# A four-layer FNet and GeGLU kernel in split fp32: the planner's price of short DMA packets, a normalisation begun one step earlier, and another layout of stored weight pieces

## Chip, cores and metric

The kernel runs on one core of a Trainium2 chip. The metric is the device time of one execution in microseconds. Before the change three runs took 1600.6, 1602.94 and 1600.12 us, a median of 1600.6 us. A profile of one more execution, which itself took 1600.54 us, is the source of all rows below.

## The reference

The input x has 2048 rows of 512 fp32 numbers. Four layers follow one another, each on the layer-normed rows of the last:

```python
x = x + _A_ref(_layernorm(x), ...)   # Cr @ (z Hr) - Ci @ (z Hi), the real part of a 2-D DFT
x = x + _B_ref(_layernorm(x), ...)   # (gelu(z @ w_gate) * (z @ w_up)) @ w_down
x = x + _A_ref(_layernorm(x), ...)
x = x + _B_ref(_layernorm(x), ...)
```

Cr and Ci are 2048 x 2048, Hr and Hi 512 x 512, w_gate and w_up 512 x 1792, w_down 1792 x 512. `_layernorm` subtracts the row's mean and divides by the root of its variance plus 1e-5.

## The kernel before, in words

**Arithmetic.** Each fp32 operand is divided into a high part rounded to fp32r (`split`, L121 on ScalarE, called ACT) and a rest (L123 on VectorE, called DVE). A product is three TensorE (PE) matmuls, high by high, high by rest, rest by high (`mm3`, L161 to L163). Large products go by a Strassen scheme with seven operands in place of eight, named A11, A12, S1, S2, S3, S4 and A22; their sums and differences are the DVE lines L149 and L152.

**Stages.** Layers 0 and 2 (`mix`) go over four blocks b of 512 output rows, first all products with the sequence matrices (`fore`, S2, S4), then the products with the hidden matrices (`hid_groups`); in layer 2 blocks 2 and 3 do the latter together (`pair_products`). Layers 1 and 3 (`geglu`) go twice, for w = 0 and w = 1, over 1024 rows each: 14 steps `up(n)` of seven products make gate and up, then the products with w_down follow. A product in `up` is six matmuls and calls `step()` once.

**Buffers.** All tiles of 128 x 512 come from 93 slots handed out in turn (`sb`, named s in the profile); two wide tiles, `wide` and `xwide`, hold four such tiles each and serve at times as slots, at times for turned rows. PE writes to eight PSUM banks (p).

**Weights that are kept.** Weight sums are made once, divided, and stored to DRAM by POOL (GpSimd's queue), so that later passes load them ready. `weight_steps` makes four pieces for each block of gate and up (DRAM tiles wb), of w_down (wc, `wdd`) and of the paired hidden matrices (wp, `whd`). A piece is a pair of operands such as S2 and S3, each of 256 columns: `split_slot` makes one tile with both operands' high parts and one with both rests, and `kept` (L274) stores these two tiles one behind the other, 2 KB a row each. A w_down or wp load (`piece_of`, L262, issued by SyncE's queue, SP, at L293) wants one operand, high and rest, so it reads two runs of 1 KB a row. The loads of wb (`piece_load`, L1021) take the whole tiles as they were stored. The fourth piece holds S4 alone, high beside rest. w_down's blocks 0 to 2 are made in the first mix layer beside block 0's hidden products, the others in the first GeGLU pass (`up`, L1090); wh's own pieces (whs) are stored by `kept` as well.

**Normalisation.** In layer 0 the terms come from DVE and one POOL instruction (L511); in the others `norm_terms` has ACT sum and square the row (L518 to L520), POOL make 1/root (L521, L522) and ACT the shift (L523); then L540 on ACT writes the normalised row. For the GeGLU layers `block_steps` does this for eight tiles of 128 rows per w: `norm(i)` loads rows ahead (`x_load_mixed`, L198, SP), normalises tile i, lets DVE transpose it into `wide` (L624), and after each fourth tile POOL stores `wide` to DRAM (t, L627); `fetch` (L638) loads it back in runs of 512 bytes. For w = 0 these steps run as chores beside the hidden products of blocks 1 and 2 (in layer 2 of block 2's as queue entries); for w = 1 they lie in `slow`, of which every ninth `step()` runs one (PACE), during the GeGLU pass for w = 0. `terms_ahead` makes the terms alone for layer 2's first rows, with the scratch tile `junk`.

**Turned rows.** `load_turned` (L229, SP) loads rows of x into `wide` or `xwide` in runs of 512 bytes, products are added to them, and `rows_done` (L242, POOL) stores them.

**Order.** The code's order is a priority; which instruction stands where on each engine is fixed at build time by a planner that runs a timing model of the machine. `machine_as_traced` sets four of that model's constants from traces: the gap between matmuls, SP's delay, the depth of the issue queues, and 21.5 bytes per ns for each DMA engine. At run time each engine and each queue works in the planned order and waits at its head.

Of the kernel before, what the change touches and what calls it, by code (L numbers as in the profile page):

```python
# [9 lines left out]
F32 = mybir.dt.float32  # L10
# [4 lines left out]
P = 128  # L15
S, D, F = 2048, 512, 1792
# [5 lines left out]
NT = TB // P  # L22
# [28 lines left out]
SP_DELAY_NS = 3000  # L51
DEPTH = 1
DMA_BYTES_PER_NS = 21.5


@with_exitstack
def fnet_geglu(ctx: ExitStack, tc: tile.TileContext, x_in, ws, wh, whc, wgu, wdc, out):
    nc = tc.nc
# [5 lines left out]
    tpool = ctx.enter_context(tc.tile_pool(name="turned", bufs=1))  # L64
# [11 lines left out]
    junk = cpool.tile([P, D], F32, name="junk")  # L76
# [36 lines left out]
    sb = Slots(slots, "s", NSLOT)  # L113
    ps8 = Slots(psum, "p", 8)

    def f32(ap):
        return ap.bitcast(F32)
# [74 lines left out]
    def x_load_mixed(layer, i):  # L192

        g, n = divmod(i, NT)
        t = sb.get()
        for j in range(NT):
            r0 = j * P + n * 32
            nc.sync.dma_start(t[j * 32:(j + 1) * 32], xs[layer, g][r0:r0 + 32])  # L198
        return t
# [62 lines left out]
    def piece_of(place, k, name):  # L262

        i = next(i for i, names in enumerate(pieces) if name in names)
        needs[len(items)] = place[k].name, i
        if i == 3:
            return place[k][:, 3 * 1024:]
        h = half[pieces[i].index(name)]
        return place[k][:, i * 1024:(i + 1) * 1024].rearrange("p (h c) -> p h c", h=2)[:, :, h]

    def halves(t):
        return t[:, :512], t[:, 512:]

    def kept(place, parts):  # L274
        for t, a in zip(parts, halves(place)):
            nc.gpsimd.dma_start(a, f32(t))  # L276


    items, needs, outside = [], {}, set()
# [1 line left out]
    raws, parts = {}, {}  # L281
# [206 lines left out]
    known, terms_made = {}, []  # L488

    def row_of(layer, i, mixed):  # L490
        x = fresh.pop(("mixed", i) if mixed else i, None)
        if x is None:
            x = (x_load_mixed if mixed else x_load)(layer, i)
        return x
# [31 lines left out]
    def terms_ahead(layer, i, n):  # L526
# [6 lines left out]
        known[layer, i] = norm_terms(layer, i, x, junk)  # L533
        sb.put(x)

    def normed(layer, i, mixed=False):
        x = row_of(layer, i, mixed)
        z = sb.get()
        rstd, shift = known.pop((layer, i), None) or norm_terms(layer, i, x, z)
        nc.scalar.activation(z, x, AF.Identity, bias=shift, scale=rstd)  # L540
        sb.put(x)
        return z
# [5 lines left out]
    def first_norm(layer, k):  # L548
        za[k] = normed(layer, k)
# [56 lines left out]
    def block_steps(layer, w):  # L606

        zt, t, wide = {}, {}, {}
        turned = [dram.tile([P, NT * D], F32, name=f"t{layer}_{w}_{part}") for part in range(2)]

        def norm(i):

            def run():
                r0 = w * 2 * NT
                end = 2 * NT if w else i // NT * NT + NT
                for k in range(i if i == 0 or i + NT == end and not w else i + 2, min(i + 3, end)):
                    fresh["mixed", r0 + k] = x_load_mixed(layer, r0 + k)
                z = normed(layer, r0 + i, True)
                part, n = divmod(i, NT)
                if n == 0:  # L620
                    assert not sb.out("z")
                    wide[part] = tpool.tile([P, NT * D], F32, name="wide")
                to = wide[part].rearrange("p (b n t) -> p b n t", n=NT, t=32)
                nc.vector.transpose(to[:, :, n], z.rearrange("p (b t) -> p b t", t=32))  # L624
                sb.put(z)
                if n == NT - 1:
                    nc.gpsimd.dma_start(turned[part], wide.pop(part))  # L627
            return run

        def fetch(c):  # L630

            def run():
                for part in range(2):
                    v = zt[c, part] = sb.get()
                    for i in range(P // 32):
                        cols = turned[part][:, (c * 4 + i) * P:(c * 4 + i + 1) * P]
                        to = v[i * 32:(i + 1) * 32]
                        nc.sync.dma_start(  # L638
                            to.rearrange("p (j t) -> p j t", t=P), cols.rearrange("(j p) t -> p j t", p=32)
                        )  # L640
            return run

        def difference(a, b):
            v = sb.get()
            minus(v, a, b)
            return v

        def first(c):
            def run():
                v = t[f"B{1 + c // 2}1", c % 2] = zt.pop((c, 0))  # L650
                blocks[f"B{1 + c // 2}1", c % 2] = split_slot(v)
            return run

        def second(c):
            def run():
                v = zt.pop((c, 1))
                if c < 2:
                    t["B12", c] = v
                    t["T1", c] = difference(v, t["B11", c])
                    sb.put(t.pop(("B11", c)))  # L660
                else:
                    c0 = c - 2
                    t["T2", c0] = difference(v, t["T1", c0])
                    t["T3", c0] = difference(v, t["B12", c0])
                    sb.put(t.pop(("B12", c0)))
                    blocks["B22", c0] = split_slot(v)
                    sb.put(v)
            return run

        def fourth(c):  # L670
            def run():
                t["T4", c] = difference(t["B21", c], t["T2", c])
                sb.put(t.pop(("B21", c)))
            return run

        def divide(name, c):
            def run():
                blocks[name, c] = split_slot(t[name, c])
                sb.put(t.pop((name, c)))
            return run  # L680

        one = [norm(i) for i in range(2 * NT)]
        two = [fetch(c) for c in range(ND)] + [first(c) for c in range(ND)] + [second(c) for c in range(ND)]
        two += [fourth(c) for c in range(2)]
        two += [divide(name, c) for name in ("T2", "T3", "T1", "T4") for c in range(2)]
        return one, two
# [272 lines left out]
    wblocks = {n: dram.tile([P, 7 * 512], F32, name=f"wb{n}") for n in range(NF)}  # L959
# [3 lines left out]
    def weight_steps(n, raw=wgu, place=wblocks):  # L963

        src, v = [], {}

        def load():
            src.extend(sb.get() for _ in range(4))
            for i, names in enumerate((*pieces[:3], ("S4", "A21"))):
                for name, h in zip(names, half):  # L970
                    v[name] = src[i][:, h]
            with tc.issue_after(stream["last"].ins):
                nc.sync.dma_start(src[0], raw[n, :, :512])
                nc.sync.dma_start(v["A22"], raw[n, :, 512:768])
                nc.sync.dma_start(v["A21"], raw[n, :, 768:])

        def sums():
            plus(v["S1"], v["A21"], v["A22"])
            minus(v["S2"], v["S1"], v["A11"])
            minus(v["S3"], v["A11"], v["A21"])  # L980
            minus(v["S4"], v["A12"], v["S2"])

        def divide(i):
            def run():
                to = place[n][:, i * 1024:min((i + 1) * 1024, 7 * 512)]
                if i < 3:
                    t = split_slot(src[i])
                    kept(to, t)
                else:
                    t = (split_side(v["S4"]),)  # L990
                    nc.gpsimd.dma_start(to, f32(t[0]))
                if place is wblocks:
                    piece_here(n, i, t)
                else:
                    outside.add((place[n].name, i))
                    sb.put(*t)
                sb.put(src[i])
            return run

        return load, [sums] + [divide(i) for i in range(len(pieces))]  # L1000
# [375 lines left out]
@contextmanager  # L1376
def machine_as_traced():

    from concourse import hw_specs

    spec = hw_specs.TRN2Spec
    kept = {name: getattr(spec, name) for name in ("PE_FULL_CLOCK_PASS_GAP_NS", "DGE_DMA_DELAY", "ENG_ISSUE_QUEUE_DEPTH", "DMA_BUS_BYTES_PER_NS_PER_ENGINE")}
    spec.PE_FULL_CLOCK_PASS_GAP_NS = PASS_GAP_NS
    spec.DGE_DMA_DELAY = {**spec.DGE_DMA_DELAY, mybir.EngineType.SP: SP_DELAY_NS}
    spec.DMA_BUS_BYTES_PER_NS_PER_ENGINE = DMA_BYTES_PER_NS
    depth = {mybir.EngineType.DVE: DEPTH, mybir.EngineType.Activation: DEPTH}
    spec.ENG_ISSUE_QUEUE_DEPTH = {**spec.ENG_ISSUE_QUEUE_DEPTH, **depth}
    try:
        yield
    finally:  # L1390
        for name, value in kept.items():
            setattr(spec, name, value)
# [47 lines left out]
```

## Time and profile before

| what | value |
|---|---|
| median of three runs | 1600.6 us (1600.12 to 1602.94) |
| profiled execution | 1600.54 us, span 1598.8 us |
| PE busy, granted clock | 99% of the span, 0.999 |
| DVE, ACT, POOL busy | 77%, 54%, 14% |
| DMA | 422.85 MB, mean 264 GB/s |
| HBM read, written | 339.74 MB, 81.53 MB |

The span runs from the first to the last instruction that the profile has; the execution's own time is 1.7 us more. In rows of a timeline the columns are start, duration, engine, line, operation, tiles and, in brackets, how long the engine stood idle ahead of it and for whom. In a table of windows each row has the window, its length, busy time and starts for PE, PE's weight loads, DVE, ACT and POOL, then the granted clock, the share of the 16 DMA engines and GB/s. In rows by line, three durations are least, median and largest in ns, followed by the first and the last start. A DMA row of a window ends with the size and the median time from issue to landing; a queue's row has packets, MB and its share of the 16 engines. A share over 1.00 means that packets waited for one another.

### The profile page before, as it was taken

Reading aid. Unit: us, or ns where it says so; the run is one execution under the profiler, and the core shown is the slowest. Engines: PE = TensorE matmul, PEld = TensorE weight load, DVE = VectorE, ACT = ScalarE, POOL = GpSimd, SP = SyncE. Lnnn points to the kernel's source line nnn. Section 1 sums busy time; section 2 is a strip of 40 time slices with the busy share of each in tenths; the row PEclk is TensorE's granted clock in tenths of the full one; section 3 lists DMA queues with packets and bytes.
Section 4 is the critical chain, followed back from the end, with each engine's and each line's share of the span. In section 5 each row is a group of like instructions: output and inputs, shape, how many; then the busy total and the mean of one; then the engine's idle time right before and its main releaser. Section 6 shows DMA issues by size and latency. Waiting matters only on the chain.

```text
span 1598.8 us, 23017 instructions
## 1 busy us (share of the span) xinstructions
PE 1586.9 (99%) x7026; PEld 1313.1 (82%) x7026; DVE 1236.8 (77%) x2148; ACT 856.4 (54%) x1680; POOL 225.2 (14%) x410
## 2 busy tenths in 40 slices
PE   9999999999999999999999999999999999999998
PEld 7888788888878888788888888888888888888887
DVE  8999879789789795665869988789985548754484
ACT  7864454545666653556777435436446545433361
POOL 2212200112465201220041000001001000000000
PEclk9999999999999999999999999999999999999999
DMA  9949987787989899995967677778998967897462
GB/s 362 329 158 331 352 273 254 234 285 265 339 321 332 296 311 308 292 363 180 305 229 247 239 267 244 251 248 240 266 328 237 293 207 234 295 257 227 133 191 54
DMA packets 276379, 422.85 MB, mean 264 GB/s; under 512 B 28864, under 2 KB 131264, under 8 KB 275232
## 3 DMA queue, kind: packets, MB, share of 16 engines
q1 hardware_dynamic: 251600, 338.26, 67.0%
q0 software_dynamic: 23840, 82.73, 14.1%
q8 instruction: 56, 0.92, 0.2%
q14 instruction: 67, 0.55, 0.1%
q10 hardware_dynamic: 816, 0.39, 0.1%
HBM read 339.74 MB, written 81.53 MB: 263 GB/s over the span
## 4 chain that ended last, share of the span: by engine, by line
PE 83%; issue 12%; DMA 3%; ACT 1%; POOL 1%; DVE 0%; SPq 0%; POOLq 0%; ACTq 0%; DVEq 0%
PE p L162 28%; PE p L161 28%; PE p L163 28%; DMA s<-ws 2%; POOL rstd L521 0%; DMA wide<-x 0%; DMA s<-x 0%; ACT s L121 0%; DMA s<-wdc 0%; SPq L293 0%; ACT s L540 0%; DVE s L123 0%; DVE s L152 0%; POOL out L242 0%; ACT s L156 0%
## 5 line engine op out<-in xcount | busy, mean ns | idle before, releaser
L162 PE MATMUL p<-s,s 128*128 128x512 f32 (+1 forms) x2334 | 903.2, 388 | 1.1 <-DVE s L123 1.1
L163 PE MATMUL p<-s,s 128*128 128x512 f32 (+1 forms) x2334 | 891.9, 388 | 0.0
L161 PE MATMUL p<-s,s 128*128 128x512 f32 (+1 forms) x2334 | 874.9, 388 | 2.0 <-ACT s L156 1.5
L121 ACT ACTIVATE s<-s 128x512 fp32r<-128x512 f32 (+1 forms) x834 | 467.6, 607 | 344.4 <-DVE s L149 125.3
L123 DVE TENSOR_TENSOR s<-s,s 128x512 fp32r<-128x512 f32 (+1 forms) x834 | 521.2, 660 | 56.1 <-ACT s L121 53.9
L161 PEld LDWEIGHTS p<-s,s 128*128 128x128 f32 x2334 | 438.2, 188 | 94.6 <-ACT s L121 2.4
L162 PEld LDWEIGHTS p<-s,s 128*128 128x128 f32 x2334 | 438.4, 188 | 92.4 <-DVE s L123 2.6
L163 PEld LDWEIGHTS p<-s,s 128*128 128x128 f32 x2334 | 438.2, 188 | 89.7
L152 DVE TENSOR_TENSOR s<-s,p 128x512 f32<-128x512 f32 x290 | 194.8, 682 | 197.8 <-PE p L163 114.1
L149 DVE TENSOR_TENSOR s<-s,s 128x512 f32<-128x512 f32 (+1 forms) x403 | 242.3, 617 | 7.2 <-DMA s<-ws 4.9
L156 ACT ACTIVATE s<-p 128x512 f32<-128x512 f32 x246 | 143.8, 592 | 142.2 <-PE p L163 141.3
L1035 ACT ACTIVATE s<-s 128x512 f32<-128x512 f32 x112 | 70.1, 629 | 120.8 <-DVE s L152 120.1
L521 POOL TENSOR_SCALAR rstd<-rstd 128x1 f32<-128x1 f32 x48 | 18.6, 387 | 356.7 <-ACT s L520 271.3
L1049 DVE TENSOR_TENSOR s<-s,s 128x512 f32<-128x512 f32 x84 | 57.8, 688 | 1.7
L276 POOL DMA_DIRECT2D wb<-s x84 | 45.5, 544 | 88.7 <-ACT s L121 64.0
L121 ACT ACTIVATE s<-xwide 128x512 fp32r<-128x512 f32 (+1 forms) x66 | 39.8, 615 | 27.8 <-DVE xwide L149 14.6
L152 DVE TENSOR_TENSOR s<-s,s 128x512 f32<-128x512 f32 (+1 forms) x69 | 40.2, 586 | 15.6 <-DMA s<-ws 6.1
L540 ACT ACTIVATE s<-s,shift,rstd 128x512 f32<-128x512 f32 x59 | 47.6, 810 | 4.6 <-DVE shift L512 4.0
L123 DVE TENSOR_TENSOR s<-xwide,s 128x512 fp32r<-128x512 f32 (+1 forms) x66 | 44.0, 673 | 4.0 <-ACT s L121 3.1
L242 POOL DMA_DIRECT2D out<-wide x8 | 5.2, 655 | 287.1 <-DVE wide L152 182.2
L242 POOL DMA_DIRECT2D x<-wide x12 | 7.8, 659 | 234.1 <-DVE wide L152 234.1
L624 DVE STREAM_TRANSPOSE wide<-s 128x512 f32<-128x512 f32 x31 | 21.8, 705 | 20.3 <-ACT s L540 17.6
(121 smaller groups left out, 520.7 us busy)
## 6 DMA issues: line engine op xcount, KB each, us to landing
s<-ws SPq DMA_DIRECT2D x361, 256.0 KB, 5.1
s<-wb SPq DMA_DIRECT2D x294, 256.0 KB, 5.5
s<-wc SPq DMA_DIRECT2D x196, 256.0 KB, 4.8
wb<-s POOLq DMA_DIRECT2D x98, 256.0 KB, 5.8
s<-wh SPq DMA_DIRECT2D x85, 256.0 KB, 5.0
xwide<-ws SPq DMA_DIRECT2D x55, 256.0 KB, 4.5
s<-x SPq DMA_DIRECT2D x54, 256.0 KB, 4.5
wc<-s POOLq DMA_DIRECT2D x49, 256.0 KB, 6.0
```

The lines of the kernel that those rows point to most:

```text
L121: nc.scalar.activation(hi, src, AF.Copy)
L123: nc.vector.tensor_tensor(lo, src, f32(hi), op=ALU.subtract)
L149: nc.vector.tensor_tensor(out, a, b, op=ALU.subtract)
L152: nc.vector.tensor_tensor(out, a, b, op=ALU.add)
L156: nc.scalar.activation(v, src, AF.Copy)
L161: nc.tensor.matmul(ps, ah, bh, start=start, stop=False, skip_group_check=True)
L162: nc.tensor.matmul(ps, ah, bl, start=False, stop=False, skip_group_check=True)
L163: nc.tensor.matmul(ps, al, bh, start=False, stop=stop, skip_group_check=True)
L276: nc.gpsimd.dma_start(a, f32(t))
L540: nc.scalar.activation(z, x, AF.Identity, bias=shift, scale=rstd)
L1035: nc.scalar.activation(t, g, AF.Gelu_apprx_tanh)
L1049: nc.vector.tensor_tensor(t, t, v, op=ALU.mult)
```

## The change

Three things are changed. The planner's model gets a fifth constant, a least duration of 37 ns for a DMA packet. In `block_steps` a step takes up row i, makes its terms, and then normalises, transposes and (after the fourth) stores row i - 1; one step is added at the end for the last row, so there are nine for each w; the terms' scratch tile is now `junk` everywhere. And the first three pieces of a w_down or wp block are stored operand by operand, high beside rest, so that `piece_of` reads 2 KB in one run a row; the store writes two runs of 1 KB. wb and whs are stored as before.

```diff
+DMA_PACKET_NS = 37
...
         h = half[pieces[i].index(name)]
-        return place[k][:, i * 1024:(i + 1) * 1024].rearrange("p (h c) -> p h c", h=2)[:, :, h]
+        return place[k][:, i * 1024 + h.start * 2:i * 1024 + h.stop * 2]
...
-    def kept(place, parts):
-        for t, a in zip(parts, halves(place)):
-            nc.gpsimd.dma_start(a, f32(t))
+    def kept(place, parts, by_name=False):
+        for n, t in enumerate(parts):
+            to, t = halves(place)[n], f32(t)
+            if by_name:
+                to = place.rearrange("p (h m c) -> p h m c", h=2, m=2)[:, :, n]
+                t = t.rearrange("p (h c) -> p h c", h=2)
+            nc.gpsimd.dma_start(to, t)
...
+    begun = {}
+
+    def norm_begun(layer, i, mixed=False):
+
+        x = row_of(layer, i, mixed)
+        begun[layer, i] = x, known.pop((layer, i), None) or norm_terms(layer, i, x, junk)
+
     def normed(layer, i, mixed=False):
-        x = row_of(layer, i, mixed)
+        if (layer, i) not in begun:
+            norm_begun(layer, i, mixed)
+        x, (rstd, shift) = begun.pop((layer, i))
         z = sb.get()
-        rstd, shift = known.pop((layer, i), None) or norm_terms(layer, i, x, z)
         nc.scalar.activation(z, x, AF.Identity, bias=shift, scale=rstd)
...
-                z = normed(layer, r0 + i, True)
-                part, n = divmod(i, NT)
...
+                norm_begun(layer, r0 + i, True)
+                if i:
+                    turn(i - 1)
             return run
+
+        def turn(i):
+
+            z = normed(layer, w * 2 * NT + i, True)
+            part, n = divmod(i, NT)
...
+            nc.vector.transpose(to[:, :, n], z.rearrange("p (b t) -> p b t", t=32))
+            sb.put(z)
+            if n == NT - 1:
+                nc.gpsimd.dma_start(turned[part], wide.pop(part))
...
-        one = [norm(i) for i in range(2 * NT)]
+        one = [norm(i) for i in range(2 * NT)] + [lambda: turn(2 * NT - 1)]
...
-                    kept(to, t)
+                    kept(to, t, place is not wblocks)
...
+    spec.DMA_MIN_TRANSFER_TIME = DMA_PACKET_NS
```

More of the change, by code (lines that the diff above doesn't have):

```diff
@@ L617, in run @@
                     fresh["mixed", r0 + k] = x_load_mixed(layer, r0 + k)
-                z = normed(layer, r0 + i, True)
-                part, n = divmod(i, NT)
[L620 to L627, printed above, removed]
-            return run
+                norm_begun(layer, r0 + i, True)
+                if i:
+                    turn(i - 1)
+            return run
+        def turn(i):
+            z = normed(layer, w * 2 * NT + i, True)
+            part, n = divmod(i, NT)
+            if n == 0:
+                assert not sb.out("z")
+                wide[part] = tpool.tile([P, NT * D], F32, name="wide")
+            to = wide[part].rearrange("p (b n t) -> p b n t", n=NT, t=32)
+            nc.vector.transpose(to[:, :, n], z.rearrange("p (b t) -> p b t", t=32))
+            sb.put(z)
+            if n == NT - 1:
+                nc.gpsimd.dma_start(turned[part], wide.pop(part))
         def fetch(c):
@@ L1381, in machine_as_traced @@
     spec = hw_specs.TRN2Spec
-    kept = {name: getattr(spec, name) for name in ("PE_FULL_CLOCK_PASS_GAP_NS", "DGE_DMA_DELAY", "ENG_ISSUE_QUEUE_DEPTH", "DMA_BUS_BYTES_PER_NS_PER_ENGINE")}
+    kept = {name: getattr(spec, name) for name in ("PE_FULL_CLOCK_PASS_GAP_NS", "DGE_DMA_DELAY", "ENG_ISSUE_QUEUE_DEPTH", "DMA_BUS_BYTES_PER_NS_PER_ENGINE", "DMA_MIN_TRANSFER_TIME")}
     spec.PE_FULL_CLOCK_PASS_GAP_NS = PASS_GAP_NS
```

## The prediction

> **What bounds the kernel now.** I read the totals of the page first, then the table of busy time by windows of 100 us, then the waits of PE, and last the timeline around each place where PE stood still.
>
> ```profile
> PE 1586.9 (99%) x7026; PEld 1313.1 (82%) x7026; DVE 1236.8 (77%) x2148; ACT 856.4 (54%) x1680; POOL 225.2 (14%) x410
> ```
> ```profile
> 0.00:100.00 100.00, 98.35 (x431) 81.68 (x432) 93.44 (x221) 78.41 (x147) 19.89 (x34) 1.00 0.89 314
> 100.00:200.00 100.00, 98.92 (x433) 80.58 (x432) 92.49 (x161) 49.23 (x88) 22.03 (x41) 1.00 0.84 299
> ...
> 400.00:500.00 100.00, 98.95 (x437) 81.58 (x436) 83.96 (x162) 66.75 (x143) 52.20 (x88) 1.00 0.97 331
> 500.00:600.00 100.00, 100.00 (x443) 82.81 (x442) 86.67 (x149) 61.27 (x116) 19.19 (x36) 1.00 0.91 309
> 600.00:700.00 100.00, 99.31 (x436) 81.19 (x435) 58.01 (x98) 50.12 (x114) 23.10 (x44) 1.00 1.00 305
> ...
> 1500.00:1599.00 99.00, 91.41 (x443) 77.22 (x441) 61.08 (x100) 36.33 (x67) 3.15 (x5) 0.98 0.41 119
> ```
> PE is the bound: busy in 99% of the span, at a granted clock of 1.00. A matmul's end is modelled, so I count starts (the number behind x). A full window holds 443, like 500 to 600, one start per 0.226 us. The middle windows that are not full miss 10 (100 to 200), 6 (400 to 500) and 7 (600 to 700) of them. At 0.226 us that is 2.3, 1.4 and 1.6 us; I call these stalls A, B and C. Together they are 5.3 us, 0.33% of the span. The ten windows not shown are full. The first 100 us hold the wait for the first rows, and the last window ends with the output's stores; the change touches neither.
>
> ```profile
> PE p L161 <- ACT s L156: 1.5, 2, 1.1
> PE p L162 <- DVE s L123: 1.1, 2, 0.8
> ```
> These are the two large waits of PE between 150 us and the end (total, times, longest): for copies out of its banks and for divided weights. So the whole question is what becomes of A, B and C, and whether new ones open. No gain on DVE, ACT or DMA counts in itself.
>
> **The change part by part.** *The picture.* The planner now takes at least 37 ns for a packet. At its 21.5 bytes per ns that touches packets under 37 x 21.5 = 795 bytes, which here are the 512-byte runs of the turned rows and of the fetches of t.
>
> ```profile
> s<-wc SPq DMA_DIRECT2D x196, 256.0 KB, 4.8
> s<-x SPq DMA_DIRECT2D x54, 256.0 KB, 4.5
> xwide<-x SPq DMA_DIRECT2D x38, 256.0 KB, 8.7
> wide<-x SPq DMA_DIRECT2D x20, 256.0 KB, 7.8
> ```
> 256 KB in 512-byte runs are 32 packets for each of 16 engines: planned before at 32 x 23.8 = 0.76 us, now at 32 x 37 = 1.18 us, 0.42 us more. The trace is on the side of the new picture: such loads land after 7.8 to 8.7 us, loads in longer runs after 4.5 to 4.8. The edit costs no instruction; it reorders them. The first transfers that it prices anew come late:
>
> ```profile
> L638 SPq DMA_DIRECT2D s<-t x128: 302/424/1772, 328.4 to 1339.2; - x128
> L521 POOL TENSOR_SCALAR rstd<-rstd x48: 181/190/4725, 215.6 to 1280.7; 128x1 f32<-128x1 f32 x48
> ```
> The first fetch of t is at 328.4 us, and the first of the normalisations that are begun ahead at 215.6 us (the opening's use L511). A planner that runs forward in time orders what stands before 200 us as now. Stall A stays, unless the third edit moves it.
>
> *The pieces.* A load of a piece of w_down or wh now reads one run of 2 KB a row in place of two of 1 KB, and a store of the first three pieces of a block writes two of 1 KB in place of one of 2 KB. The price of a run comes from two stretches:
>
> ```profile
> s<-wb SPq DMA_DIRECT2D x15, 256.0 KB, 5.6
> s<-wc SPq DMA_DIRECT2D x14, 256.0 KB, 5.6
> q1 hardware_dynamic: 5353, 7.43, 105.7%
> ```
> ```profile
> q1 hardware_dynamic: 1645, 2.99, 81.0%
> ```
> The first fence is 560 to 580 us: queue 1 moves 7.43 MB in 105.7% of 20 us, 0.351 MB/us, half of it wc (1 KB runs), half wb (2 KB). The second is 140 to 150 us, ws alone (2 KB runs): 2.99 MB in 8.1 us, 0.369 MB/us. A transfer of 0.262 MB takes 0.710 us there, and 0.747 us in the mixture; so one in 1 KB runs takes 0.78 us, 0.07 us more. That is the gain of each wc load, and my value for the loss of each store. For a store the trace shows no such run, so the bounds are: 0 from below, as no row has shorter runs go faster, and from above the dearest traffic there is, 620 to 640 us with its 512-byte runs:
>
> ```profile
> 140.00:150.00 10.00, 10.00 (x46) 8.29 (x45) 9.55 (x19) 6.20 (x12) 4.10 (x8) 1.00 1.02 385
> 620.00:640.00 20.00, 20.00 (x90) 16.57 (x89) 10.50 (x16) 10.32 (x28) 1.48 (x4) 1.00 1.12 293
> ```
> 385 GB/s at a share of 1.02 give 0.69 us for 256 KB, 293 at 1.12 give 1.00: 0.31 us more. I take 0.07, the row with the runs in question.
>
> Where does it meet the path? In A. There a ws load lands after twice its usual time, in a stretch where DMA is full, and POOL's stores hold most of it:
>
> ```profile
> 176.75 10.15 DMA s<-ws
> ```
> ```profile
> 165.00:170.00 5.00, 5.00 (x24) 4.13 (x23) 4.02 (x8) 2.12 (x5) 2.52 (x5) 1.00 1.03 386
> 180.00:185.00 5.00, 4.77 (x22) 3.64 (x20) 1.89 (x4) 0.67 (x2) 0.00 (x0) 1.00 1.03 394
> ```
> ```profile
> L276 POOL DMA_DIRECT2D wc<-s x14: 539/539/542, 157.0 to 173.7; - x14
> q0 software_dynamic: 772, 2.53, 63.0%
> ```
> Fourteen stores of the kind that changes go out between 157.0 and 173.7 us, and in 170 to 180 us the store queue has 63.0% of the engines. Before 165 us DMA has slack that takes up a part; for some nine stores after it I charge 9 x 0.07 = **+0.6 us** on A (bounds 0 and 14 x 0.31 = +4.3). The 224 loads of wc and wp get 0.07 us cheaper each, 15.7 us of DMA in all, but PE waits for none of them: **0**. Their cover is the lead of the loads; without it the gain would be these 0.07 us a load.
>
> The Trainium skill ("DMA: Bandwidth & Descriptors", Specifications) puts the least transfer for full rate at 512 bytes; by it 1 KB and 2 KB runs cost alike, A keeps its 2.3 us, and the sum below would be 0.6 us lower. The two stretches above speak against it by 0.07 us a transfer.
>
> *The normalisation.* Row i's terms (L518 to L523) stay in step i; its normalised row (L540, ACT) and transpose (L624, DVE), and after the fourth row the store of the part, move a step back. Nothing is added but one step, and no wait. The row keeps its buffer a step longer and its normalised copy takes one later, so one buffer of 93 more is out at a time; loads go through them in turn, and I charge nothing, the lead of the loads being the cover and the slower rival below the price without it. This bears on B:
>
> ```profile
> 471.74 4.72 POOL L521 TENSOR_SCALAR rstd<-rstd 128x1 f32<-128x1 f32 x1
> ```
> ```profile
> 477.14 0.29 ACT L523 ACTIVATE shift<-mean,rstd 128x1 f32<-128x1 f32 x1 [3.17 <-POOL rstd L522]
> ...
> 477.87 0.80 ACT L540 ACTIVATE s<-s,shift,rstd 128x512 f32<-128x512 f32 x1
> 478.57 0.57 ACT L156 ACTIVATE s<-p 128x512 f32<-128x512 f32 x1
> ```
> ```profile
> 475.40 1.01 DVE L149 TENSOR_TENSOR s<-s,s 128x256 f32<-128x256 f32 x2
> 478.70 0.71 DVE L624 STREAM_TRANSPOSE wide<-s 128x512 f32<-128x512 f32 x1 [2.28 <-ACT s L540]
> ```
> A POOL instruction that takes 0.19 us at the median took 4.72 us and ended at 476.46, when DVE's run without a gap ended (476.41). ACT stood 3.17 us at L523, and behind it in ACT's order were a division, L540 and the copy L156 that frees PE's bank. The edit takes L540 out of that line, and DVE's wait of 2.28 us for it; it does not take L523 out, which still waits for POOL in the same step. So of B's 1.4 us I take away L540's 0.8, cautiously **-0.7 us** (bounds: -1.4, all of it; and +1.4, a second such place, as 2 of 48 runs of L521 were longer than 1 us now).
>
> The Trainium skill ("SBUF — State Buffer", Who interferes with whom) has a DVE instruction with two SBUF inputs shut out a GpSimd one that reads SBUF, and nothing in the edit prevents that. By it alone B would stay whole and the sum be 0.7 us higher; the 4.72 us above agree with it.
>
> *Stall C* comes from rows whose code is not changed, only their place:
>
> ```profile
> L518 ACT ACTIVATE junk<-s x8: 613/623/633, 633.1 to 693.0; 128x512 f32<-128x512 f32 x8
>   DMA s<-x: 5.3, 1
> 654.80 6.06 DMA s<-x
> xwide<-x SPq DMA_DIRECT2D x7, 256.0 KB, 8.6
> ```
> ACT stood 5.3 us at L518 for a row issued at 654.80 that took 6.06 us. In 630 to 660 us seven of the newly priced loads are in front (last row); 7 x 0.42 = 2.9 us more in the plan lets ACT do other work first. I take **-1.0 us** of 1.6 (bounds -1.6 and +1.6, as a reordering can also put another row in such a place).
>
> **The sum.** +0.6 - 0.7 - 1.0 + 0 = -1.1 us. The profiled execution took 1600.54 us with a span of 1598.8; the median of the three runs is 1600.6, so the one stands for the others. 1600.5 - 1.1 = **1599.4 us**.
>
> **The rivals.** *Faster: all three stalls go.* If the planner's order is new from the start, A can go too: 1600.5 - 5.3 = 1595.2 us. For it: the first transfers need not be re-priced for a global order to differ. Against it: B's POOL wait and A's full DMA are still there. This is also the floor: below it lies only PE's stream. Chance 0.22; with A left, the best is 1597.5.
>
> *Slower: SP stands still behind the later store.* The last row's transpose now comes a step later, and a step is nine products of six matmuls, 54 x 0.226 = 12.2 us. Behind it hangs the store t<-wide and behind that SP:
>
> ```profile
> SPq L229 <- DMA t<-wide: 9.1, 1, 9.1
> 506.89 0.54 POOL L627 DMA_DIRECT2D t<-wide  x1
> ```
> SP waited 9.1 us with the turned-row load at its head and the wc and wgu loads behind it; PE paid nothing (500 to 600 us is full). If the planner leaves the load where it is, SP stands 9.1 + 12.2 = 21.3 us. The weights are loaded three blocks ahead but divided one block after the load, that is 7 x 6 x 0.226 = 9.5 us; from there it decides. Between no loss and 21.3 - 9.5 = 11.8 us the middle is 5.9: 1606.4 us. For it: SP's order is fixed, and this wait is there already. Against it: the planner knows the store's new place. Chance 0.28.
>
> *The change does not do what it says:* the order stays much as it is and no stall moves: 1600.5 us, chance 0.10.
>
> **How the numbers follow.** Forecast 0.40, nothing 0.10, faster 0.22, slower 0.28. A measurement of this kernel tells about 0.2%, 3.2 us, from no change; forecast and nothing lie inside that, so faster 0.22, same 0.50, slower 0.28. The forecast's own range, 1597.4 to 1602, lets two of its terms go to either end. The range reaches to the two outer cases, which together hold half: 1595.5 to 1606.5.
>
> **What would show it.** Right: the windows 400 to 500 and 600 to 700 hold more than 437 and 436 starts, 100 to 200 still about 433; L624 has no wait on L540; L523's waits on L522 remain near 10 us. Wrong: a new window below 440 starts (look at SP's waits before it), or 100 to 200 full, which would mean that the order is new from the start.

## The result, and the profile after

Thirteen runs of each kernel on one chip gave 1602.0 us (1600.02 to 1603.95) before and **1597.61 us** (1596.91 to 1599.85) after, a ratio of 0.9971 with a 95% interval of 0.9964 to 0.9979: 0.29% faster, with 4.4 us between the medians. The two profiled executions took 1600.54 and 1597.56 us, 3.0 us apart. Two executions are left out of all ratios below: one of the kernel before that took 5146 us, and the profiled one of rows_early, which took 1674 us at a granted clock of 0.90. Line numbers moved: L121 is now L122, L123 L124, L152 L153, L156 L157, L161 to L163 are L162 to L164, L229 L230, L276 L281, L293 L298, L518 to L523 are L523 to L528, L540 L553, L624 L644 and L627 L647.

The same table of windows as before the change:

```profile
100.00:200.00 100.00, 98.10 (x429) 79.93 (x428) 92.61 (x160) 49.09 (x87) 25.41 (x41) 1.00 0.82 296
...
400.00:500.00 100.00, 100.00 (x443) 82.81 (x442) 84.18 (x161) 68.37 (x147) 51.70 (x90) 1.00 0.97 333
500.00:600.00 100.00, 100.00 (x443) 82.81 (x442) 87.03 (x151) 60.60 (x112) 20.08 (x35) 1.00 0.92 318
600.00:700.00 100.00, 100.00 (x443) 82.81 (x442) 58.98 (x99) 51.13 (x115) 27.55 (x45) 1.00 0.97 307
```

Stalls B and C are gone: 437 and 436 starts have become 443 and 443. A is still there, 429 starts in place of 433. PE's waits say the same. Of the 2.7 us that it waits for a division (L122), 1.8 lie near 185 us and 0.9 in the first 150 us; the wait for L1317 is in the opening. After 192 us PE has no wait in this list:

```profile
PE p L162 <- ACT s L122: 2.7, 4, 1.6
PE p L1317 <- POOL ident masks.py:199: 1.4, 1, 1.4
```

A's chain is what it was. DVE waits for a ws load in a full DMA, ACT for DVE, PE for ACT; first DVE, then PE:

```profile
184.03 0.69 DVE L153 TENSOR_TENSOR s<-s,s 128x512 f32<-128x512 f32 x1 [2.93 <-DMA s<-ws]
```
```profile
186.02 0.73 PE L162 MATMUL p<-s,s 128*128 128x512 f32 x2 [1.60 <-ACT s L122]
```

The DMA queue of the loads carried the same bytes in fewer packets. Before and after:

```profile
q1 hardware_dynamic: 251600, 338.26, 67.0%
```
```profile
q1 hardware_dynamic: 227024, 338.26, 66.0%
```

The 24,576 packets fewer are one for each of 128 rows of 192 loads: of the 224 loads of w_down and wh, the 32 of S4 read one run a row already. 67.0% of 1598.8 us less 66.0% of 1595.8 us is 18 us of the 16 engines, but not all of it comes from the layout, since packets also wait for one another: in picture_alone below, with the old layout and all 251,600 packets, the share is 66.1%. Adding the layout to each of the four pairs of kernels below takes 18, 11, 3 and 10 us off the queue's packets, 10 on the mean, or 0.05 us for each of the 192 loads. No step of PE's became shorter by it, as the experiments show.

### The profile page after: what moved, and what is told of

Its sections match the earlier page's. It is cut to its first block, busy times and chain, and to the rows that moved or that the text cites. A ratio compares the mean times of both kernels' runs of the same rounds, so it can differ in the third digit from the quotient of the medians.

```text
span 1595.8 us, 23078 instructions
## 1 busy us (share of the span) xinstructions
PE 1585.2 (99%) x7026; PEld 1312.0 (82%) x7026; DVE 1236.1 (77%) x2148; ACT 857.9 (54%) x1680; POOL 235.9 (15%) x410
## 4 chain that ended last, share of the span: by engine, by line
PE 93%; DVE 3%; DMA 2%; issue 1%; ACT 1%; SPq 0%; POOL 0%; DVEq 0%; ACTq 0%; POOLq 0%
PE p L163 31%; PE p L164 31%; PE p L162 31%; DVE s L124 2%; DMA s<-ws 1%; DVE s L150 1%; ACT s L122 0%; DMA xwide<-ws 0%; DVE s L153 0%; DMA wc<-s 0%; DMA xwide<-wh 0%; SPq L298 0%; ACT s L553 0%; DVE st L512 0%; DVE xwide L150 0%
## 5 line engine op out<-in xcount | busy, mean ns | idle before, releaser
L163 PE MATMUL p<-s,s 128*128 128x512 f32 (+1 forms) x2334 | 902.2, 388 | 0.1
L164 PE MATMUL p<-s,s 128*128 128x512 f32 (+1 forms) x2334 | 891.5, 388 | 0.0
L162 PE MATMUL p<-s,s 128*128 128x512 f32 (+1 forms) x2334 | 874.1, 388 | 3.0 <-ACT s L122 2.7
L122 ACT ACTIVATE s<-s 128x512 fp32r<-128x512 f32 (+1 forms) x839 | 471.7, 608 | 341.6 <-DVE s L150 115.1
L124 DVE TENSOR_TENSOR s<-s,s 128x512 fp32r<-128x512 f32 (+1 forms) x839 | 526.5, 661 | 64.9 <-ACT s L122 55.6
L162 PEld LDWEIGHTS p<-s,s 128*128 128x128 f32 x2334 | 438.0, 188 | 95.6 <-ACT s L122 5.1
L163 PEld LDWEIGHTS p<-s,s 128*128 128x128 f32 x2334 | 438.2, 188 | 90.7 <-DVE s L124 0.9
L164 PEld LDWEIGHTS p<-s,s 128*128 128x128 f32 x2334 | 438.2, 188 | 89.8
L153 DVE TENSOR_TENSOR s<-s,p 128x512 f32<-128x512 f32 x291 | 195.4, 682 | 205.1 <-PE p L164 112.2
L150 DVE TENSOR_TENSOR s<-s,s 128x512 f32<-128x512 f32 (+1 forms) x411 | 247.0, 616 | 8.4 <-PE p L163 3.0
L157 ACT ACTIVATE s<-p 128x512 f32<-128x512 f32 x246 | 143.6, 593 | 150.0 <-PE p L164 140.5
L281 POOL DMA_DIRECT2D wb<-s x84 | 46.7, 564 | 120.2 <-ACT s L122 89.9
L153 DVE TENSOR_TENSOR s<-s,s 128x512 f32<-128x512 f32 (+1 forms) x73 | 42.9, 591 | 8.9 <-DMA s<-ws 5.9
L122 ACT ACTIVATE s<-xwide 128x512 fp32r<-128x512 f32 (+1 forms) x61 | 36.8, 616 | 23.8 <-DVE xwide L150 5.1
L553 ACT ACTIVATE s<-s,shift,rstd 128x512 f32<-128x512 f32 x58 | 46.2, 806 | 4.2 <-DVE shift L517 4.1
L526 POOL TENSOR_SCALAR rstd<-rstd 128x1 f32<-128x1 f32 x48 | 15.4, 320 | 222.4 <-ACT junk L525 221.9
L124 DVE TENSOR_TENSOR s<-xwide,s 128x512 fp32r<-128x512 f32 (+1 forms) x61 | 40.5, 674 | 2.3 <-ACT s L122 2.2
L523 ACT ACTIVATE junk<-s 128x512 f32<-128x512 f32 x43 | 26.8, 624 | 22.4 <-DMA s<-x 22.2
```

The costliest lines, as they stand in the source:

```text
L122: nc.scalar.activation(hi, src, AF.Copy)
L124: nc.vector.tensor_tensor(lo, src, f32(hi), op=ALU.subtract)
L150: nc.vector.tensor_tensor(out, a, b, op=ALU.subtract)
L153: nc.vector.tensor_tensor(out, a, b, op=ALU.add)
L157: nc.scalar.activation(v, src, AF.Copy)
L162: nc.tensor.matmul(ps, ah, bh, start=start, stop=False, skip_group_check=True)
```

## The experiments

Each was timed against the kernel before on the same chip. A **stall** below is again counted in missing matmul starts, or as the time that PE lost between two starts.

### Undoing one edit, and the picture alone

Theory 1 was that of the prediction, each stall with an edit of its own; theory 2, that any new order removes B and C.

```diff
-DMA_PACKET_NS = 37
+DMA_PACKET_NS = 7          # no_picture: the planner's own value
```


> The changed kernel with the planner's least packet duration put back to 7 ns; normalisation begun ahead and the new layout stay. Theory 1 (each stall has its own edit: the picture took away stall C, the normalisation stall B, the layout lengthened A): C is back at 600 to 700 us, 6 or 7 matmul starts missing there, 1.4 to 1.6 us over the changed kernel, ratio to the kernel before about 0.998; 400 to 500 full. Theory 2 (any new order does away with B and C, which were accidents of one order): both windows full, time equal to the changed kernel within 0.5 us, ratio about 0.997.

```diff
-                norm_begun(layer, r0 + i, True)
-                if i:
-                    turn(i - 1)
+                turn(i)            # no_begun; eight steps, terms made in normed
```


> The changed kernel with row i normalised and transposed in the step that makes its terms, as before; picture and layout stay. Theory 1: B is back at 400 to 500 us, some 6 starts missing, 1.4 us over the changed kernel, ratio about 0.998; 600 to 700 full. Theory 2: both windows full, ratio about 0.997.

```diff
-        return place[k][:, i * 1024 + h.start * 2:i * 1024 + h.stop * 2]
+        return place[k][:, i * 1024:(i + 1) * 1024].rearrange("p (h c) -> p h c", h=2)[:, :, h]
...
-                    kept(to, t, place is not wblocks)
+                    kept(to, t)    # no_layout
```


> The changed kernel with the pieces of w_down and wh stored as before (two runs of 1 KB for a load, one of 2 KB for a store); picture and normalisation stay. Theory 1: B and C stay away and A (100 to 200 us) goes back from 429 to 433 starts, 0.9 us below the changed kernel, ratio about 0.9965. Theory 2: A as in the changed kernel (429 starts), since its length comes from the order alone, ratio about 0.997. If the cheaper loads were what took C away, C is back and the ratio about 0.998.

`picture_alone` has both of the last two edits and the constant of 37.

> The kernel before with the least packet duration of 37 ns alone. Theory 1: C gone (600 to 700 us full), A and B as before (433 and 437 starts), 1.6 us below the kernel before, ratio about 0.999. Theory 2: B and C both gone although the normalisation is as before, 3.0 us below, ratio about 0.998.

### The other two alone

After those four, theory 3: the picture alone makes the gain.

> The kernel before with normalisation begun a step ahead alone. Theory 3 (formed after the first four runs: the picture alone makes the gain, since it lets the plan issue rows ahead of turned-row loads; the two other edits only move stalls about): a stall at which ACT waits for a row of x remains somewhere after 200 us, ratio 0.999 to 1.002. Theory 2 (any new order does away with B and C): windows after 200 us full, ratio 0.998 or lower.

> The kernel before with the pieces of w_down and wh stored operand by operand alone. Theory 3: B and C, or stalls like them, remain, and A is as long or longer, ratio 0.999 to 1.002. Theory 2: windows after 200 us full, ratio 0.998 or lower. If the cheaper loads relieved DMA where C is, C is gone and B stays, ratio about 0.999.

The eight combinations, with the starts that the profiled execution has in three windows (443 or 442 is full):

| picture | begun | layout | run | ratio to before (95%) | 400 to 500 | 600 to 700 | 1200 to 1300 |
|---|---|---|---|---|---|---|---|
| - | - | - | before | 1 | 437 | 436 | 443 |
| - | yes | - | begun_alone | 1.0006 (0.9995 to 1.0016) | 443 | 429 | 423 |
| - | - | yes | layout_alone | 0.9998 (0.9989 to 1.0008) | 437 | 425 | 442 |
| - | yes | yes | no_picture | 1.0011 (0.9999 to 1.0023) | 443 | 439 | 424 |
| yes | - | - | picture_alone | 0.9969 (0.9959 to 0.9980) | 443 | 442 | 443 |
| yes | - | yes | no_begun | 0.9974 (0.9965 to 0.9983) | 443 | 443 | 443 |
| yes | yes | - | no_layout | 0.9975 (0.9965 to 0.9986) | 443 | 443 | 443 |
| yes | yes | yes | after | 0.9971 (0.9964 to 0.9979) | 443 | 443 | 443 |

Every kernel with the picture is 0.25 to 0.31% faster and every one without it within 0.11% of the kernel before. The other two edits change nothing that these intervals tell. Two windows of interest are not in the table: in that of A the eight kernels have between 417 starts (no_begun) and 436 (layout_alone), and from 800 to 900 us no_layout has 438, a new stall of 0.8 us between two starts. Theory 2 falls: the orders of begun_alone, layout_alone and no_picture are new as well, and C is in all of them. Theory 1 falls for the time, though not in each part. Begun ahead does take B away without the picture (443 in begun_alone and no_picture, 437 in layout_alone). But with begun ahead and no picture a larger stall opens, D, at 1260 us: 20 starts are missing in begun_alone and 19 in no_picture, 4.5 and 4.3 us. D in no_picture, on ACT and then on SP:

```profile
1252.20 0.60 ACT L157 ACTIVATE s<-p 128x512 f32<-128x512 f32 x1 [2.12 <-PE p L164]
1258.53 0.63 ACT L523 ACTIVATE junk<-s 128x512 f32<-128x512 f32 x1 [5.74 <-DMA s<-x]
```
```profile
1247.23 4.21 SPq L1044 DMA_DIRECT2D s<-wb  x5
1251.80 2.29 SPq L199 DMA_DIRECT2D s<-x  x4
```

ACT stands 5.74 us at the first instruction on one of four rows that SP issued only from 1251.80 on. PE, out of free banks, loses 2.2 us between two starts, and most of the rest to a lower clock right after (last section). That is C's mechanism at another place. C itself in no_picture, the wait shortened to 4.77 us:

```profile
659.37 0.63 ACT L523 ACTIVATE junk<-s 128x512 f32<-128x512 f32 x1 [4.77 <-DMA s<-x]
```

With the picture alone, the row at which ACT stood goes out sooner. SP and ACT in picture_alone:

```profile
647.38 0.32 SPq L190 DMA_DIRECT2D s<-x  x1
...
653.03 0.49 SPq L190 DMA_DIRECT2D s<-x  x1
```
```profile
658.00 0.62 ACT L523 ACTIVATE junk<-s 128x512 f32<-128x512 f32 x1
...
663.52 0.62 ACT L523 ACTIVATE junk<-s 128x512 f32<-128x512 f32 x1
```

The built programs tell which row is which. In the kernel before, SP first issues the row that ACT takes second (at 651.47) and then, at 654.80, the row that ACT takes first and stands at. In picture_alone the latter goes out first, at 647.38, 7.4 us sooner; ACT takes it up at 658.00 and the other at 663.52, and waits for neither. So it is in all eight kernels: in the four without the picture the two rows go out in the wrong order, and the one that is needed first leaves between 653.98 and 656.87 us; in the four with it they go out in ACT's order, and it leaves between 644.65 and 649.55 us.

The change of order begins late. SP's first 355 transfers are the same in the traces of picture_alone and the kernel before, up to 351 us, and in the built programs no engine's order differs ahead of 343 us. The first fetch of t, the first transfer in 512-byte runs, goes out at 328.4 us.

### How much the packet costs

```diff
-DMA_PACKET_NS = 37
+DMA_PACKET_NS = 30         # packet_30; 60 in packet_60
```
In the trace of the kernel before, the 46,080 packets of 512 bytes took 37 ns on the mean and 27 at the median.

> The changed kernel with a least packet duration of 30 ns in place of 37: a 512-byte packet planned at 30 rather than 23.8. If pricing them nearly right is enough, no stall over 1 us after 200 us, ratio 0.997 to 0.998. If it needs the full price, ACT's wait for a row returns at 660 or 1260 us, ratio 0.999 to 1.001.

0.9979 (0.9969 to 0.9990): three quarters of the gain in the middle value, though the interval overlaps that of 37. C is still there with 4 starts missing (439): the two rows go out in the right order, but the first leaves at 651.01 us and ACT waits for it. Another stall, of 1.4 us between two starts, stands at 850 us.

> The changed kernel with a least packet duration of 60 ns in place of 37. It also prices runs of 1 KB, which the picture at 37 ns does not (60 x 21.5 = 1290 bytes). If the gain comes from pricing 512-byte packets as they are, an overpriced plan leaves the stalls after 200 us away as well but may issue weights later than it need: ratio 0.997 to 0.998. If the gain was an accident of one order, a further order brings stalls of 1 to 2 us back after 200 us: ratio 0.998 to 1.000.

1.0147 (1.0134 to 1.0161): 1625.85 us, far from what any theory expected. A price of 60 ns also raises runs of 1 KB. PE waits in many places, most of all in these three windows:

```profile
500.00:600.00 100.00, 95.98 (x413) 76.46 (x412) 87.17 (x154) 60.89 (x112) 24.18 (x42) 1.00 0.90 312
700.00:800.00 100.00, 93.37 (x394) 75.10 (x394) 72.55 (x126) 57.90 (x111) 15.07 (x23) 0.95 0.79 271
800.00:900.00 100.00, 94.39 (x405) 75.96 (x404) 74.97 (x144) 70.95 (x159) 21.09 (x39) 0.98 0.69 230
```

DMA is no busier there than in the changed kernel (shares of 0.92, 0.79 and 0.73), and the loads move the same bytes, so more traffic does not explain these waits. That they come from a plan that expects more traffic is likely but not shown, and so is which of its orders does the harm. The gain at 37 ns is at any rate not one of general caution.

### Rows loaded a step sooner

The sharper form of theory 3, tested without the picture:

```diff
-        if i == 0:
-            fresh["terms"] = x_load(layer, 0)
-        x = fresh.pop("terms")
-        if i + 1 < n:
-            fresh["terms"] = x_load(layer, i + 1)
+        for k in range(i if i == 0 else i + 2, min(i + 3, n)):
+            fresh["terms", k] = x_load(layer, k)
+        x = fresh.pop(("terms", i))
...
-                for k in range(i if ... else i + 2, min(i + 3, end)):
+                for k in range(i if ... else i + 3, min(i + 4, end)):
```


> The kernel without the picture (7 ns; normalisation begun ahead, new layout) with the rows that are summed ahead loaded one step sooner: four mixed rows in flight in place of three, and three rows in place of two for the terms of layer 2. Theory 3 in its sharper form (the stalls after 200 us that the picture cures are ACT standing at the sum of a row that has not landed): those at 660 to 670 and at 1240 to 1266 us go, and the time is near that of the changed kernel, ratio 0.997 to 0.999. Rival: the picture works through other parts of the order (weights, turned rows); the stalls stay or move, ratio 1.000 to 1.002.

0.9992 (0.9979 to 1.0005), with runs from 1596.3 to 1606.5 us. No comparable profile shows what became of its stalls. The result lies between the two theories and decides nothing: it stays open whether an earlier load alone cures these stalls.

### Stall A: fewer stores in the full stretch

```diff
-BEFORE = {0: (0, 1, 2)}
+BEFORE = {1: (0, 1, 2)}        # stores_later
+BEFORE = {0: (0,), 1: (1, 2)}  # split_12
+BEFORE = {0: (0, 1), 1: (2,)}  # split_21
```


> The changed kernel with w_down's blocks 0 to 2 made and stored beside block 1's hidden products in place of block 0's, so that their stores lie after 200 us. If POOL's stores in a full DMA make stall A, the window 100 to 200 us misses at most 3 starts in place of 14, and the time falls by up to 2.5 us, ratio about 0.9955. Rival: the ws and m loads fill DMA there by themselves; A stays within 1 us, ratio about 0.997, or a new stall opens at 200 to 230 us, where the stores now are.

0.9998 (0.9990 to 1.0007). A is gone altogether, as expected, but the time did not fall: a larger stall stands where the stores now are, as the rival had it, though near 259 us:

```profile
100.00:200.00 100.00, 100.00 (x443) 82.81 (x442) 91.48 (x151) 46.05 (x80) 10.75 (x20) 1.00 0.73 251
200.00:300.00 100.00, 95.84 (x411) 78.46 (x411) 78.78 (x137) 55.70 (x118) 24.95 (x40) 0.97 0.82 279
```

There ACT again stands at rows that have not landed:

```profile
251.68 0.63 ACT L523 ACTIVATE junk<-s 128x512 f32<-128x512 f32 x1 [4.75 <-DMA s<-x]
...
257.57 0.63 ACT L523 ACTIVATE junk<-s 128x512 f32<-128x512 f32 x1 [3.18 <-DMA s<-x]
```

> The changed kernel with w_down's blocks 0 and 1 made beside block 0's hidden products and block 2 beside block 1's. If A grows with POOL's stores in the full stretch, a third fewer of them shorten A from 2.7 to about 1 us, and block 1's stretch (a stall of 6.4 us with all three there) takes one block without loss: ratio about 0.996. Rival: a loss opens at 250 to 270 us as large as what A gives back, ratio 0.997 to 0.999.

> The changed kernel with block 0 of w_down made beside block 0's hidden products and blocks 1 and 2 beside block 1's. By the same reasoning A goes (0 to 0.5 us), and a stall at 250 to 270 us opens, of 0 to 4 us: ratio 0.9955 to 0.999. The rival, that A comes from the loads alone, was answered by the run with all three later; what is told apart is how many stores each stretch takes.

split_12 gave 0.9987 (0.9978 to 0.9995): A gone, 418 starts in 200 to 300 us and 431 in 300 to 400. **split_21 gave 0.9950 (0.9938 to 0.9962), 1595.25 us, the fastest of all kernels here**, with five runs within 1.1 us of one another:

```profile
100.00:200.00 100.00, 100.00 (x443) 82.81 (x442) 95.30 (x163) 50.04 (x89) 20.62 (x34) 1.00 0.79 284
200.00:300.00 100.00, 100.00 (x442) 82.80 (x442) 80.19 (x136) 52.34 (x115) 16.27 (x28) 1.00 0.83 279
300.00:400.00 100.00, 100.00 (x440) 82.17 (x439) 88.81 (x150) 48.84 (x89) 14.13 (x26) 1.00 0.78 256
```

Moving a third of these stores is enough to end A, and moving two thirds or all opens another stall. That the stores were what slowed A's loads shows in the window from 165 to 185 us, first in the changed kernel, then in stores_later:

```profile
q0 software_dynamic: 1383, 4.57, 59.0%
s<-ws SPq DMA_DIRECT2D x8, 256.0 KB, 8.2
```
```profile
q0 software_dynamic: 320, 1.05, 13.8%
s<-ws SPq DMA_DIRECT2D x9, 256.0 KB, 5.2
```

POOL's queue (q0) takes 59.0% of the engines in the one and 13.8% in the other, and a ws load lands after 8.2 and 5.2 us. But a full DMA alone does not make the stall. In split_21 the ws loads of this window still land after 7.7 us, DMA has a share of 1.04 to 1.06 from 170 to 190 us, and PE waits for nothing. The edit moves the blocks' loads and divisions too and gives SP another order; which of these ends A there was not separated.

## Why the prediction was right, and where it was not

The time lies in the range (1595.5 to 1606.5), 1.8 us below the forecast. The likeliest class, within 0.2%, was not the one that came: the change is faster by 0.29%. That the time came so near the forecast is in part luck: the start of the sum was 1.5 us too low (1600.5 for a median of 1602.0) and the change 3.3 us too small (-1.1 for -4.4), and these two errors partly cancel. The profiled execution, 1597.56 us, is the case that the prediction called the best with A left, 1597.5.

- **PE as the bound, and A, B and C as the whole question.** Right: no row of another engine explains anything of the difference.
- **The picture's reach.** Right: with the picture alone no order ahead of 343 us is moved, and the first fetch of t is at 328.4 us.
- **Stall C, -1.0 us.** Right in kind, too small: all of it went in every kernel with the price of 37, 1.6 us in the profiled execution, and in layout_alone C was 18 starts, over 4 us. The prediction saw the newly priced loads ahead of the row and expected ACT to do other work first. What it did not see is that SP also had the two rows in the wrong order, and that the picture would put them right and send the needed one 7.4 us sooner.
- **Stall B, -0.7 us.** This step failed in its reading of causes. I gave B to the normalisation alone. The normalisation does take all of it away, but so does the picture without it, and without the picture the edit opens D, 4.3 us in no_picture. The sum had only "a second such place" of up to 1.4 us, meant as another long run of L521; D is a wait for a row instead. What goes with B is not L540's 0.8 us on ACT but the long POOL instruction: in picture_alone and no_begun L540 (L553) keeps its place right after the terms, and B is gone. Of the eight kernels of the table, B stands in the two where that run of L521 (L526) takes over 4.5 us, the kernel before (4.72) and layout_alone (4.56), and in none of the others, whose longest run between 440 and 560 us takes 1.95. In layout_alone, then in picture_alone:

```profile
471.56 4.56 POOL L526 TENSOR_SCALAR rstd<-rstd 128x1 f32<-128x1 f32 x1
```
```profile
473.53 0.77 POOL L526 TENSOR_SCALAR rstd<-rstd 128x1 f32<-128x1 f32 x1
```

  Why the run is shorter in the other orders was not tested.
- **L523's wait for POOL** stayed, as foretold (near 10 us): 10.1 us before, 10.9 after. **L624's wait for L540** did not go, against the forecast, though it fell from 17.6 us to 10.6; both after the change:

```profile
  POOL rstd L527: 10.9, 15
```
```profile
  ACT s L553: 10.6, 7
```

- **Stall A, +0.6 us for the stores.** Not borne out. A lost 10 starts before and 14 after in the profiled executions, 2.3 and 3.2 us, which looks like it; but with the new layout the kernels with the same stores, packet_30 and packet_60 among them, have 417 to 436 starts in that window, and with the old layout the four have 429 to 434. Even one order varies so: the kernel before and picture_alone have the same order up to 343 us, and one execution of each had 433 and 429 starts. Nor did the stores take more of the DMA engines. Before and after:

```profile
q0 software_dynamic: 23840, 82.73, 14.1%
```
```profile
q0 software_dynamic: 23840, 82.73, 14.2%
```

  The packets of POOL's queue are as many as before, so the 0.07 us that I charged each store, from loads in shorter runs, has no counterpart there. What did grow is the issue on POOL, which I had not priced, 707 to 729 ns a store in place of 539 to 542:

```profile
L281 POOL DMA_DIRECT2D wc<-s x14: 707/714/729, 158.1 to 174.3; - x14
```

- **The loads, 0.07 us each and worth nothing to PE.** Right in the main: 0.05 us on the mean of four pairs, for the 192 loads that changed and not 224, and layout_alone is at 0.9998.
- **SP behind the later store.** The rival did not come. SP's wait grew from 9.1 to 11.2 us; the store t<-wide went out at 509.72, 2.8 us later and not 12.2, and PE's window 500 to 600 us is full:

```profile
SPq L230 <- DMA t<-wide: 11.2, 1, 11.2
```
```profile
509.72 0.54 POOL L647 DMA_DIRECT2D t<-wide  x1 [0.94 <-DVE wide L644]
```

- **The size.** Besides B and C, the start of the sum was mis-sized. I let the profiled execution (1600.54 us) and three runs (1600.6) stand for the kernel before; thirteen and more runs put its median at 1602.0 to 1602.9. Of the 3.0 us between the two profiles, B and C are 1.4 and 1.6, A takes back 0.9 and the first 100 us 0.2. About 1.2 us lie behind the start of the last matmul (7.6 us to the end before, 6.5 after), where no edit acts and the kernels here differ by as much. Where the remaining 1.4 us between the medians come from no profile shows; longer stalls in the other executions of the kernel before would explain them.

## What to carry to other kernels

Where a planner fixes the order, an underpriced transfer shows up as an engine standing at the head of its queue for data that the plan believed there; look for such waits (here ACT at the first sum of a row) before changing the work itself, and see in which order the queue sends what the engine will need. Price the transfer as measured (37 ns was the mean of the 512-byte packets in the trace): too little (7 ns) and too much (60 ns) both lost, here 0.4% (no_picture) and 1.8% (packet_60) against 37. An edit that removes one stall is to be tried with each other edit taken away, since begun ahead cured B and opened D, and D was gone with the picture. And when PE is 99% busy, count the starts that are missing in each window: what is left to gain stands there. Moving a third of some stores gave another 0.2% on top of the three edits (split_21).

## What the runs showed of the hardware

The granted TensorE clock falls after quite a short wait. After the stall at 185.8 us in no_begun, in which PE lost 2.3 us between two starts, the clock granted is 0.50 from 188.77 to 192.18 us, and matmuls start every 427 ns:

```profile
185.36:188.77 3.41, 1.25 (x6) 0.74 (x5) 2.39 (x4) 1.66 (x3) 0.00 (x0) 1.00 1.04 410
188.77:192.18 3.41, 3.41 (x10) 2.66 (x9) 3.41 (x7) 2.46 (x6) 0.00 (x0) 0.50 1.04 401
```

After the one at 184.0 us in the changed kernel, 1.8 us, it stays at 1.00:

```profile
186.10:190.00 3.90, 3.70 (x15) 2.64 (x16) 3.90 (x8) 2.95 (x6) 0.00 (x0) 1.00 1.04 401
```

D in no_picture (2.2 us) is of the first kind as well:

```profile
1259.29:1262.70 3.41, 1.45 (x6) 1.23 (x7) 1.39 (x3) 2.95 (x8) 0.74 (x2) 1.00 0.95 307
1262.70:1266.11 3.41, 3.41 (x9) 2.64 (x9) 1.20 (x2) 0.81 (x3) 0.00 (x0) 0.50 1.03 377
```

Over the thirteen profiles other than that of rows_early, and after the first 100 us, stalls of up to 1.9 us at the full clock were never followed by it, and of nine from 2.2 us on eight were; one of 2.7 us in layout_alone was not. The traces' records of the clock say why. A stretch at half clock lasts 3.41 us, or two or three times that, and in one run all of them begin on one grid of 3.41 us steps: in packet_60 at 183.06, 732.60 and 875.96 us, 161 and 42 steps apart. What counts is how much PE loses within one step. In these profiles a step at the full clock that lost 1.96 us or more was always followed by a step at half clock, and one that lost 1.93 us or less never. The stall in layout_alone is cut by the grid into 1.9 and 0.9 us:

```profile
661.06:664.47 3.41, 1.69 (x8) 1.07 (x6) 0.24 (x1) 1.52 (x4) 0.00 (x0) 1.00 0.79 240
664.47:667.88 3.41, 2.62 (x10) 1.79 (x11) 3.41 (x8) 3.41 (x11) 2.10 (x4) 1.00 0.66 213
```

Seven or eight matmuls at 427 ns cost another 1.4 to 1.6 us, so a wait just over 2 us that falls into one step costs PE nearly twice its length. The Trainium skill ("TensorE: Matmul & The Clock Gate", Part 1) has the clock halved after an idle window of about 3.4 us; half the clock and the 3.41 us agree, but here a step did not have to be idle throughout. It fits that kernels without the picture also vary more from run to run (no_picture 1599.9 to 1610.3 us, picture_alone 1596.3 to 1599.0), but that was not traced run by run.
